# Two moves in a pipelined loop: one block transpose behind the last low part of h, and the fourth output scatter of each half step into that step

## The chip, the cores and the metric

The kernel runs on one core of a Trainium2 chip. The metric is device time in microseconds (us), from the start to the end of one launch. Before the change the median of three runs is 740.99 us (740.6 to 742.04). The engines are named as in the profile: PE (TensorE matmul), PEld (its weight loads), DVE (VectorE), ACT (ScalarE), POOL (GpSimd, which issues the DMAs that gather or scatter rows by an index list) and SP (which issues the plain DMAs).

## The reference

The reference has two parts. The first is an attention over columns; its result, read as 20,224 tokens of 256 features, goes into a routed two-layer network with 8 experts.

```python
def _attn_ref(q, k, v, tau):                      # q, k, v: 4 x 5056 x 256
    qn = q / (np.linalg.norm(q, axis=1, keepdims=True) + 1e-06)
    kn = k / (np.linalg.norm(k, axis=1, keepdims=True) + 1e-06)
    s = kn.transpose(0, 2, 1) @ qn / tau
    s = s - s.max(-1, keepdims=True)
    a = np.exp(s)
    a /= a.sum(-1, keepdims=True) + 1e-09
    return (v @ a).astype(np.float32)

def _moe_ref(x, w_skip, w_gate, w1, w2):          # x: 20224 x 256, F = 1024
    do_compute = x @ w_skip > 0
    out = x.copy()
    xc = x[do_compute]
    logits = xc @ w_gate
    e_idx = np.argmax(logits, axis=1)
    gate_w = ...                                  # softmax of logits at e_idx
    for e in range(8):
        mask = e_idx == e
        h = np.maximum(xc[mask] @ w1[e], 0.0)
        y[mask] = gate_w[mask, None] * (h @ w2[e])
    out[do_compute] = xc + y
    return out
```

The change concerns only the last part: for chunks of tokens of one expert, `h = relu(x w1)`, `y = h w2`, and `out = x + gate * y`, written back to the rows that the tokens came from.

## The kernel before

The attention, the routing and the first nine chunks of the network run ahead of the loop that the change touches. Their order is written by a planner (a table of costs and due times); the nine chunks run "ahead", between the products of the attention. Then comes `Large.loop()`, with five passes of two chunks each. A chunk is 512 tokens of one expert in four tiles (t = 0 to 3) of 128 tokens. A last loop for small remainders makes no pass here.

A chunk goes through these steps. `take` copies its index list, `gather` fetches its 512 rows into `xg` with four indirect DMAs from POOL (`gather_tile`, L235). `turned` makes two block transposes of `xg` into `xt` on DVE (L320), one for each half of the 256 features; SP writes them to a scratch in memory and reads them back as `xT` (`moved_out`, L323, and `moved_in`, L326), and `split_x` splits `xT` into a high and a low part, `xH` and `xL`. `first` computes `ph = x w1` for eight blocks f of 128 hidden features (three matmuls for each of two feature halves, L380 to L382). For each f ACT writes the high part `hH` (L385) and DVE the low part `hL` (L386). `second` computes for each tile t the product with `w2`: eight matmuls with `hH` (L406), then eight with `hL` (L408). DVE multiplies by the gate and adds `x` (L413, L414) into the buffer `xg[2]`, and `put(2, t)` scatters the 128 rows of the tile to `out` with one indirect DMA from POOL (L240). The index list that the puts read is a copy of its own, `lc[2]`, made by `take_out` on POOL (L426).

A pass has four stages. Stages 0 and 1 hold `first` of half 1 (all in `first(True, 1)`, in which the second weights are split as well) and `second(0, t)`; stages 2 and 3 hold `first(False, 0)` and `second(1, t)`. So the halves are offset: while one half is in `second`, the list and rows for another are already fetched. Before each `tc.stage_boundary()` every engine has a place in its program called `behind(...)`. An engine enters the next stage only when all five engines have come past their `behind` in the stage ahead of it. The program has a semaphore for each of the four boundaries. PE's first matmul of `second(1, 0)` waits for the semaphore `sem_stage_1`, to which POOL contributes behind `take_out(1)` in stage 2. Between stages an engine runs its own instructions in the order in which they are written; POOL is a single queue of takes, gathers, puts and weight gathers (`gather_w`, L247), each waiting for what it needs.

In the kernel before, three of the four puts of a half step stand in the stage in which the tile is computed, except in stage 1, which holds all four; the fourth put of `second(1, t)` is `put_last()`, and stands in stage 0 of the next pass, behind the four gathers. After the last pass one more `put_last()` stands behind the loop. The last of the nine chunks ahead has three puts in the planner's table, and its fourth is the `put_last()` of the first pass. In `first`, for h = 0, both block transposes (`turned`) stand between the matmuls of the last block, f = 7, and its `first_h`, so DVE runs them ahead of the last `hL`. For h = 1 they stand behind everything.

Of the kernel before, what the change touches and what calls it, by code (L numbers as in the profile page):

```python
# [29 lines left out]
NFB = F // P  # L30
# [9 lines left out]
K0 = 9  # L40
# [121 lines left out]
def attn_moe(ctx: ExitStack, tc: tile.TileContext, q, k, vt, tau, w_skip, w_gate, w1, w2, out):  # L162
# [95 lines left out]
    def behind(*engines):  # L258

        for e in engines:  # L260
            tc.previous_stage_wait(e.engine)
# [7 lines left out]
    class Large:  # L269
# [118 lines left out]
        def first(self, new, h):  # L388

            for f in range(NFB):  # L390
                ph = psum["h"].tile([P, 512], F32, name="ph")
                self.first_p(ph, f)
                if f == NFB - 1 and h == 0:
                    self.turned(h)
                self.first_h(ph, f)
                if new and f < 4:
                    self.split_w2(f)
                if f == 4:
                    behind(T, S, V)
            if h == 1:  # L400
                self.turned(h)
# [127 lines left out]
        def loop(self):  # L529
            with tc.For_i(0, self.n, 1, iteration_sync="staggered", hint_engines=(mybir.EngineType.PE,)) as i, tc.manual_schedule():  # L530
                V.tensor_copy(self.wc, self.wii[:, ds(i + 1, 1)])
                V.tensor_copy(self.wd, self.wii[:, ds(i + 1, 1)])
                self.take(1)
                behind(G, SP)
                self.gather(1)
                self.put_last()
                gather_w(w1, self.w1r, self.wc)
                self.take_out(0)
                self.first(True, 1)
                tc.stage_boundary()  # L540
                self.moved_out()
                load_list(self.adi, i + 1, self.lN[:, :8, :], 8)
                gather_w(w2, self.w2r, self.wd)
                self.moved_in()
                for t in range(4):
                    self.second(0, t)
                    if t == 1:
                        behind(T, S, V, G, SP)
                        self.split_x()
                tc.stage_boundary()  # L550
                self.take(0)
                self.gather(0)
                self.take_out(1)
                behind(G, SP)
                self.first(False, 0)
                tc.stage_boundary()
                self.moved_out()
                self.moved_in()
                for t in range(4):
                    if t < 2:  # L560
                        self.split_w1(2 * t)
                        self.split_w1(2 * t + 1)
                    self.second(1, t, t < 3)
                    if t == 1:
                        self.split_x()
                        behind(T, S, V, G, SP)
            self.put_last()

    class Small:

# [563 lines left out]
    for c in range(NC):  # L1134
        b, ch = divmod(c, NCH)
        ld, users = {}, ([], [])
        for h in range(2):
            for j0, j1 in [(0, 2), (2, JH)] if c == 0 and h == 0 else [(0, JH)]:
                t = then("qk", add("D", 0.76 * (j1 - j0), lambda c=c, h=h, j0=j0, j1=j1: load_qk(c, h, j0, j1), due=1e9 if c else -99, hold=("part", 99) if j0 else ("qk", NQ)))
# [26 lines left out]
        for j in range(J):  # L1166
# [3 lines left out]
            t = then("A", add("T", 0.73 if (c, j // JH) in SPLIT else 0.873, lambda g=g: next(g), deps, nominal["A", c, j]))  # L1170
# [34 lines left out]
    for d in range(NC):  # L1205
# [10 lines left out]
        for j in range(J // 2):  # L1216
            t = then("B", add("T", 1.49, None, [sv[j > 2][1], sv[j >= 2][1], ready_a[b]], nominal["B", d, j], hold=("px", 2, 1)))
# [92 lines left out]
    for x in range(K0):  # L1310
        for i in range(4):
            gt = then("gat", add("G", 1.31 if i else 1.9, lambda x=x, i=i: large.gather_ahead(x, i), [lstA if x < KA else lstB, puts.get(x - 3)]))
            gt.rush = 0.0 if x else RUSH
            gd = add("D", 0.36, None, [gt])
        gd.slack = SLACK if x else 0.0
        tr = moved_last = rows_ready(x, gd)
        if x:
            for t in tr:
                t.due = nominal["H", x - 1, 4]
        for i in range(4):  # L1320
            g = large.first_ahead(2 * i)
            t = then("H", add("T", 2.74, None, tr + w1s[1::2], nominal["H", x, i], hold=("px", 2, 1)))
            t.f = lambda g=g, t=t: product(g, t)
            t.users, a = [], None
            for n in range(2):
                a = add("S", 0.6, lambda g=g, n=n: g.send((n, 0)), [t, done.get(x - 1), a])
                t.users.append(add("V", 0.69, lambda g=g, n=n: g.send((n, 1)), [a]))
            in_order["hL", i] = t.users
        last_m1 = t
        vs2 = []  # L1330
        for i in range(2 if x < K0 - 1 else 1):
            g = large.second_ahead(x, 2 * i)
            t = then("H", add("T", 5.65, None, [v for n in range(4) for v in in_order["hL", n]] + w2s[1::2], nominal["H", x, 4 + i], hold=("px", 2, 1)))
            t.early = {id(v): 0.69 * n for n in range(4) for v in in_order["hL", n]}
            t.f = lambda g=g, t=t: product(g, t)
            t.users = chain(g, ("V", 1.92), deps=[t])
            vs2 += t.users * 2
        for i in (2, 3) if x == K0 - 1 else ():
            def alone(x=x, i=i):
                po = psum["x"].tile([P, 2, 512], F32, name="px")[:, 0, :] if i == 2 else psum["t"].tile([P, 512], F32, name="pt")  # L1340
                yield from large.second_alone(x, i, po)
            g = alone()
            t = then("H", add("T", 2.82, None, [], nominal["H", x, 5], hold=("px", 2, 1) if i == 2 else ("pt", 1)))
            t.f = (lambda g=g, t=t: product(g, t)) if i == 2 else lambda g=g: next(g)
            t.users = chain(g, ("V", 0.99), deps=[t])
            vs2 += t.users
        done[x] = t
        for i in range(4 if x < K0 - 1 else 3):
            pt = then("put", add("G", 1.31, lambda x=x, i=i: large.put_ahead(x, i), [vs2[i]], nominal["H", x, 5] + 39))
            puts[x] = add("D", 0.36, None, [pt], nominal["H", x, 5] + 41)  # L1350

# [7 lines left out]
    t = based[NC - 1]  # L1359
    for n, cost in enumerate((1.6, 1.4, 1.7, 0.77, 2.05, 0.82, 1.58, 2.81, 0.87)):  # L1360
        t = add("V", cost, table_part, [t])
# [33 lines left out]
    for at, p in enumerate(TAILS):  # L1395
# [20 lines left out]
        f = steps("tail_transposed")  # L1416
        t = add("T", 0.3, f, [tgd, wg1], nominal["T", p, 0] - 6, hold=("pt", 1))
        c = add("S", 0.4, f, [t, firsts.get(older)])
        t.users = [c]
        f = steps("tail_first")  # L1420
        t = firsts[p] = add("T", 3.5, None, [c, *tw[0]], nominal["T", p, 1], hold=("px", 2, 1))
# [4 lines left out]
        f = steps("tail_turned")  # L1426
        t = turned[p] = add("T", 0.9, None, [r1], nominal["T", p, 2], hold=("px", 2, 1))
# [4 lines left out]
        f = steps("tail_second")  # L1432
        t = tails[p] = add("T", 3.5, None, [c0, c1, *tw[1]], nominal["T", p, 3], hold=("px", 2, 1))
# [80 lines left out]
```

## Time and profile before

The profile is of one execution that took 743.1 us; its span, from the first instruction to the last, is 741.4 us.

| what | before |
|---|---|
| median of three runs | 740.99 us (740.6 to 742.04) |
| the profiled execution | 743.1 us |
| its span | 741.4 us |
| PE busy | 727.0 us, 98% of the span |
| PEld busy | 632.1 us, 85% |
| DVE busy | 516.5 us, 70% |
| POOL busy | 393.7 us, 53% |
| ACT busy | 340.1 us, 46% |
| scatters by L240 | 76 (36 of the chunks ahead, 40 of the loop) |

The busy shares are over the whole launch. The loop is its last third, from 510.5 to 734.8 us, and the shares are others there. PE's slices on the page show nine tenths or more in every slice but the first and the last, and the granted clock is at its full level throughout.

### The profile page before, as it was taken

How to read it: one execution, taken by the hardware profiler on the slowest of the kernel's cores; microseconds unless marked ns; L12 is line 12 of the kernel's file. 1: busy time of each engine (PE TensorE's matmuls, PEld its weight loads, DVE VectorE, ACT ScalarE, POOL GpSimd, SP SyncE). 2: the span in 40 equal slices, each digit the busy share in tenths (PEclk: the TensorE clock that was granted, in tenths of full speed). 3: DMA queues.
4: the chain of work that ended last, by engine and by line, in shares of the span. 5: the costliest groups of instructions: out<-in, count | busy, mean ns of one | idle time of the engine just before them, and what ended most of it. 6: DMA issues, size and time to landing. Idle time of an engine off the chain costs nothing. (4 is left out here: it accounts for less than half of the span.)

```text
span 741.4 us, 12542 instructions
## 1 busy us (share of the span) xinstructions
PE 727.0 (98%) x4234; PEld 632.1 (85%) x4234; DVE 516.5 (70%) x1022; ACT 340.1 (46%) x515; POOL 393.7 (53%) x412
## 2 busy tenths in 40 slices
PE   7999999999999999999999999999999999999996
PEld 6899999999999888988888886578888888888885
DVE  4859989988887885674746883146566675767755
ACT  5668778767847542442412222233233442334422
POOL 4000188888887777786676653324345354344542
PEclk9999999999999999999999999999999999999999
DMA  8989989899676446642525748941332223233122
GB/s 355 368 317 364 369 297 370 258 393 376 207 256 227 127 144 172 215 146 85 159 73 141 280 160 297 380 152 50 89 110 79 99 85 94 97 107 99 56 85 87
DMA packets 85188, 145.05 MB, mean 196 GB/s; under 512 B 20554, under 2 KB 60264, under 8 KB 82832
## 3 DMA queue, kind: packets, MB, share of 16 engines
q1 hardware_dynamic: 68960, 119.74, 46.4%
q0 software_dynamic: 15200, 24.00, 10.2%
q10 hardware_dynamic: 976, 0.67, 0.3%
q8 instruction: 27, 0.44, 0.2%
q14 instruction: 25, 0.20, 0.1%
HBM read 115.71 MB, written 42.70 MB: 214 GB/s over the span
## 5 line engine op out<-in xcount | busy, mean ns | idle before, releaser
L1015 POOL DMA_INDIRECT lst<-pay,r_posi x160 | 190.2, 1188 | 131.6 <-DVE r_posi L1012 79.7
L240 POOL DMA_INDIRECT out<-xg,lc x76 | 78.1, 1027 | 125.9 <-DVE xg L414 75.0
L861 PE MATMUL s<-qt,kt 128*128 128x256 f32 x580 | 136.9, 387 | 5.0 <-DMA kt<-in_k 5.0
L861 PEld LDWEIGHTS s<-qt,kt 128*128 128x128 f32 x580 | 108.9, 194 | 18.4 <-DMA kt<-in_k 5.0
L235 POOL DMA_INDIRECT xg<-out,lc x80 | 83.6, 1044 | 35.1 <-issue 28.9
L934 PE MATMUL px<-aH,vH 128*128 128x266 f32 x320 | 99.0, 309 | 0.0
L935 PE MATMUL px<-aL,vH 128*128 128x266 f32 x320 | 91.5, 286 | 0.0
L936 PE MATMUL px<-aH,vL 128*128 128x266 f32 x320 | 91.4, 286 | 0.0
L385 ACT ACTIVATE hH<-ph 128x512 fp32r<-128x512 f32 x80 | 47.8, 598 | 83.9 <-PE ph L382 83.9
L941 ACT COPY xo<-px 128x532 f32<-128x532 f32 x80 | 48.1, 602 | 70.4 <-PE px L936 69.6
L406 PE MATMUL po<-w2s,hH 128*128 128x512 f32 x320 | 79.9, 392 | 0.0
L386 DVE SCALAR_TENSOR_TENSOR hL<-ph,hH 128x512 fp32r<-128x512 f32 x80 | 55.1, 688 | 35.5 <-ACT hH L385 34.3
L489 ACT ACTIVATE hH<-px 128x512 fp32r<-128x512 f32 x72 | 39.5, 596 | 85.0 <-PE px L382 85.0
L406 PE MATMUL px<-w2s,hH 128*128 128x512 f32 x280 | 70.3, 393 | 0.0
L491 DVE SCALAR_TENSOR_TENSOR hL<-px,hH 128x512 fp32r<-128x512 f32 x72 | 46.3, 682 | 31.4 <-ACT hH L489 31.2
L406 PEld LDWEIGHTS po<-w2s,hH 128*128 128x128 f32 x320 | 58.2, 189 | 10.8
L380 PE MATMUL ph<-xH,w1H 128*128 128x512 f32 x160 | 62.5, 390 | 0.8 <-PE m L1453 0.8
L381 PE MATMUL ph<-xL,w1H 128*128 128x512 f32 x160 | 62.4, 390 | 0.0
L382 PE MATMUL ph<-xH,w1L 128*128 128x512 f32 x160 | 62.3, 389 | 0.0
L935 PEld LDWEIGHTS px<-aL,vH 128*128 128x128 f32 x320 | 60.7, 190 | 1.3
L934 PEld LDWEIGHTS px<-aH,vH 128*128 128x128 f32 x320 | 60.5, 189 | 1.2
L936 PEld LDWEIGHTS px<-aH,vL 128*128 128x128 f32 x320 | 60.3, 188 | 0.0
(252 smaller groups left out, 1397.4 us busy)
## 6 DMA issues: line engine op xcount, KB each, us to landing
vf<-in_vt SPq DMA_DIRECT2D x32, 640.0 KB, 6.1
qt<-in_q SPq DMA_DIRECT2D x31, 640.0 KB, 7.7
kt<-in_k SPq DMA_DIRECT2D x31, 640.0 KB, 7.9
out<-xo SPq DMA_DIRECT2D x12, 1280.0 KB, 6.8
turn<-xt SPq DMA_DIRECT2D x38, 256.0 KB, 2.0
xT<-turn SPq DMA_DIRECT2D x38, 256.0 KB, 3.7
v1r<-in_w SPq DMA_DIRECT2D x8, 1024.0 KB, 9.6
v2r<-in_w SPq DMA_DIRECT2D x8, 1024.0 KB, 7.3
```

What stands on the lines that cost most here:

```text
L235: apart(G.indirect_dma_start(out=to, out_offset=None, in_=out[0:n, :], in_offset=IndirectOffsetOnAxis(ap=ls[:, 0:1], axis=0), bounds_check ...
L240: i = (G.indirect_dma_start(out=out, out_offset=IndirectOffsetOnAxis(ap=ls[:, 0:1], axis=0), in_=src, in_offset=None, bounds_check=NTOK - ...
L380: T.matmul(ph, self.w1H[:, fs], self.xH[:, kb, :], start=(kb == 0), stop=False)
L381: T.matmul(ph, self.w1H[:, fs], self.xL[:, kb, :], start=False, stop=False)
L382: T.matmul(ph, self.w1L[:, fs], self.xH[:, kb, :], start=False, stop=(kb == 1))
L386: V.scalar_tensor_tensor(self.hL[:, f, :], ph, 0.0, self.hH[:, f, :], ALU.max, ALU.subtract)
L406: T.matmul(po, self.hH[:, f, ts], self.w2s[:, f, :, :], start=(f == 0), stop=False, skip_group_check=True)
L861: T.matmul(sums[b][:, cb, :], kt[:, j % JH, cb * P : (cb + 1) * P], qt[:, j % JH, :], start=(ch == 0 and j == 0 and cb == 0), stop=(ch == ...
L934: T.matmul(px[:, i, :NA], vH[:, kb, js], aH[:, kb, :], start=(kb == 0), stop=False)
L935: T.matmul(px[:, i, :NA], vH[:, kb, js], aL[:, kb, :], start=False, stop=False)
L936: T.matmul(px[:, i, :NA], vL[:, kb, js], aH[:, kb, :], start=False, stop=(kb == 1))
L1015: i = G.indirect_dma_start(out=lst, out_offset=IndirectOffsetOnAxis(ap=posi[:, t : t + 1], axis=0), in_=pay[:, d, 2 * t : 2 * t + W], in_o ...
```

## The change

Two things move, and no operation is added or taken away. The first is in `first`, for h = 0: of the two block transposes one stays ahead of the last `first_h`, and one now stands behind it. The second concerns the fourth puts. That of the first half's step, `second(0, 3)`, leaves stage 1 and stands in stage 2, behind the four gathers and ahead of `take_out(1)`. That of the second half's step, `second(1, 3)`, now stands in stage 3 with the other three, so the `put_last()` in stage 0 and the one behind the loop go. The last chunk ahead gets its fourth put in the planner's table, ahead of the loop.

```diff
--- before.py
+++ after.py
@@ -391,8 +391,10 @@
                 ph = psum["h"].tile([P, 512], F32, name="ph")
                 self.first_p(ph, f)
                 if f == NFB - 1 and h == 0:
-                    self.turned(h)
+                    self.turned_part(h, 0)
                 self.first_h(ph, f)
+                if f == NFB - 1 and h == 0:
+                    self.turned_part(h, 1)
                 if new and f < 4:
                     self.split_w2(f)
                 if f == 4:
@@ -533,7 +535,6 @@
                 self.take(1)
                 behind(G, SP)
                 self.gather(1)
-                self.put_last()
                 gather_w(w1, self.w1r, self.wc)
                 self.take_out(0)
                 self.first(True, 1)
@@ -543,13 +544,14 @@
                 gather_w(w2, self.w2r, self.wd)
                 self.moved_in()
                 for t in range(4):
-                    self.second(0, t)
+                    self.second(0, t, t < 3)
                     if t == 1:
                         behind(T, S, V, G, SP)
                         self.split_x()
                 tc.stage_boundary()
                 self.take(0)
                 self.gather(0)
+                self.put_last()
                 self.take_out(1)
                 behind(G, SP)
                 self.first(False, 0)
@@ -560,11 +562,10 @@
                     if t < 2:
                         self.split_w1(2 * t)
                         self.split_w1(2 * t + 1)
-                    self.second(1, t, t < 3)
+                    self.second(1, t)
                     if t == 1:
                         self.split_x()
                         behind(T, S, V, G, SP)
-            self.put_last()
 
     class Small:
 
@@ -1345,7 +1346,7 @@
             t.users = chain(g, ("V", 0.99), deps=[t])
             vs2 += t.users
         done[x] = t
-        for i in range(4 if x < K0 - 1 else 3):
+        for i in range(4):
             pt = then("put", add("G", 1.31, lambda x=x, i=i: large.put_ahead(x, i), [vs2[i]], nominal["H", x, 5] + 39))
             puts[x] = add("D", 0.36, None, [pt], nominal["H", x, 5] + 41)
 
```

The first place is POOL's queue at the turn from stage 1 to stage 2. `xg_152` is the buffer of results and `lc_162` the puts' index list; `xg_150` and `lc_160` are the rows and list being fetched. Names such as `DMASW4_..._stg1` are semaphores by which an earlier software DMA of that stage reports that it has landed, and `sem_stage_1` marks the boundary to stage 3. POOL before:

```order
L240 DMA out<-xg_152,lc_162 20224x256 [waits DVE_I-5912_stg1]
L530 ISA [waits sem_stage_0_7432]
L299 COPY lc_160<-lN 128x8 [waits DMAHW2_I-5912_stg1]
L235 DMA xg_150<-out,lc_160 128x256 [waits Pool_I-5912_stg2]
L235 DMA xg_150<-out,lc_160 128x256 x3
L426 COPY lc_162<-lc_161 128x8 [waits DMASW3_I-5912_stg1,DMASW4_I-5912_stg1,DMASW2_I-5912_stg1,DMASW1_I-5912_stg1]
L530 ISA [waits DMASW4_I-5912_stg1,DMASW0_I-5912_stg1,DMASW3_I-5912_stg1,DMASW1_I-5912_stg1,DMASW2_I-5912_stg1,sem_stage_1_7433]
```

POOL after, the same stretch:

```order
L240 DMA out<-xg_152,lc_162 20224x256 [waits DMASW4_I-5915_stg0,DMASW3_I-5915_stg0,Pool_I-5915_stg0,DMASW2_I-5915_stg0,DMASW0_I-5915_stg0,DMASW1_I-5915_stg0,DVE_I-5915_stg1]
L532 ISA [waits sem_stage_0_7432]
L299 COPY lc_160<-lN 128x8 [waits DMAHW2_I-5915_stg1]
L235 DMA xg_150<-out,lc_160 128x256 [waits Pool_I-5915_stg2]
L235 DMA xg_150<-out,lc_160 128x256 x2
L235 DMA xg_150<-out,lc_160 128x256 [waits DVE_I-5915_stg1]
L240 DMA out<-xg_152,lc_162 20224x256 [waits DVE_I-5915_stg1]
L428 COPY lc_162<-lc_161 128x8 [waits DMASW3_I-5915_stg1,DMASW4_I-5915_stg2,DMASW2_I-5915_stg1,DMASW1_I-5915_stg1]
L532 ISA [waits DMASW0_I-5915_stg1,DMASW3_I-5915_stg1,DMASW1_I-5915_stg1,DMASW2_I-5915_stg1,sem_stage_1_7433]
```

The fourth put has moved from ahead of the stage boundary to behind the gathers, the fourth gather has a wait for DVE that it did not have, and the copy L426 (now L428), `take_out(1)`, waits for the landing of a DMA of stage 2, the put just ahead of it, where it waited for one of stage 1.

The second place is POOL's queue at the entry of the loop. The `ISA` rows that follow the puts belong to the loop's entry, and the one with `barrier_...` is the wait for all engines. POOL before:

```order
L240 DMA out<-xg_152,lc_162 20224x256 [waits DMASW0_49,DVE_49]
L240 DMA out<-xg_152,lc_162 20224x256 [waits DMASW1_49,DVE_49]
L240 DMA out<-xg_152,lc_162 20224x256 [waits DMASW2_49,DVE_49]
L530 ISA x2
L530 ISA [waits barrier_Pool_Activation_PE_DVE_SP_gather,DMASW5_49,DMASW4_49,DMASW3_49]
```

POOL after:

```order
L240 DMA out<-xg_152,lc_162 20224x256 [waits DMASW0_49,DVE_49]
L240 DMA out<-xg_152,lc_162 20224x256 [waits DMASW1_49,DVE_49]
L240 DMA out<-xg_152,lc_162 20224x256 [waits DMASW2_49,DVE_49]
L240 DMA out<-xg_152,lc_162 20224x256 [waits DMASW3_49,DVE_49]
L532 ISA x2
L532 ISA [waits barrier_Pool_Activation_PE_DVE_SP_gather,DMASW6_49,DMASW7_49,DMASW5_49,DMASW4_49]
```

Four puts of the last chunk ahead stand there where three stood, and the entry follows behind the fourth.

The third place is DVE's queue in `first(False, 0)`, stage 2, from the first block f = 0 to the last; `xt_2575` and `xt_2576` are the two transposed halves. DVE before:

```order
L386 SCALAR_TENSOR_TENSOR hL<-ph,hH 128x512 [waits sem_stage_0_7432,Activation_I-5912_stg2]
L386 SCALAR_TENSOR_TENSOR hL<-ph,hH 128x512 [waits Activation_I-5912_stg2] x4
L386 SCALAR_TENSOR_TENSOR hL<-ph,hH 128x512 [waits DVE_I-5912_stg1,Activation_I-5912_stg2]
L386 SCALAR_TENSOR_TENSOR hL<-ph,hH 128x512 [waits Activation_I-5912_stg2]
L320 STREAM_TRANSPOSE xt_2575<-xg_150 128x4x4x32 [waits DMASW2_I-5912_stg2,DMASW1_I-5912_stg2,DMASW3_I-5912_stg2,DMASW0_I-5912_stg2,DMAHW0_I-5912_stg1]
L320 STREAM_TRANSPOSE xt_2576<-xg_150 128x4x4x32 [waits DMAHW1_I-5912_stg1]
L386 SCALAR_TENSOR_TENSOR hL<-ph,hH 128x512 [waits Activation_I-5912_stg2]
```

DVE after:

```order
L386 SCALAR_TENSOR_TENSOR hL<-ph,hH 128x512 [waits sem_stage_0_7432,Activation_I-5915_stg2]
L386 SCALAR_TENSOR_TENSOR hL<-ph,hH 128x512 [waits Activation_I-5915_stg2] x4
L386 SCALAR_TENSOR_TENSOR hL<-ph,hH 128x512 [waits DVE_I-5915_stg1,Activation_I-5915_stg2]
L386 SCALAR_TENSOR_TENSOR hL<-ph,hH 128x512 [waits Activation_I-5915_stg2]
L320 STREAM_TRANSPOSE xt_2575<-xg_150 128x4x4x32 [waits DMASW2_I-5915_stg2,DMASW1_I-5915_stg2,DMASW3_I-5915_stg2,DMASW0_I-5915_stg2,DMAHW0_I-5915_stg1]
L386 SCALAR_TENSOR_TENSOR hL<-ph,hH 128x512 [waits Activation_I-5915_stg2]
L320 STREAM_TRANSPOSE xt_2576<-xg_150 128x4x4x32 [waits DMAHW1_I-5915_stg1]
```

The last `hL` row stood behind both transposes and now stands between them.

## Rows read from the trace of the kernel before

**Rows 1.** Busy by stretch: sum, PE, PEld, DVE, ACT, POOL, clock, DMA, GB/s.

```profile
510.50:734.80 224.30, 222.18 (x1120) 188.76 (x1120) 149.06 (x248) 80.70 (x140) 97.05 (x110) 1.00 0.29 91
```

**Rows 2.** Waits of PEld in the loop: us, count, longest of one.

```profile
PEld po L408 <- DVE hL L386: 3.0, 5, 0.8
```

**Rows 3.** Timeline, PEld: start, busy, what, [idle before, releaser]; passes 4 and 5.

```profile
677.98 1.77 PEld L406 LDWEIGHTS po<-w2s,hH 128*128 128x128 f32 x8
...
681.55 0.19 PEld L408 LDWEIGHTS po<-w2s,hL 128*128 128x128 f32 x1 [0.74 <-DVE hL L386]
...
722.89 1.77 PEld L406 LDWEIGHTS po<-w2s,hH 128*128 128x128 f32 x8
```

**Rows 4.** Timeline, DVE, the end of first(False, 0) in pass 4.

```profile
678.80 2.12 DVE L320 STREAM_TRANSPOSE xt<-xg 128x512 f32<-128x512 f32 x2 [0.38 <-DMA xg<-out,lc]
680.82 0.67 DVE L386 SCALAR_TENSOR_TENSOR hL<-ph,hH 128x512 fp32r<-128x512 f32 x1
```

**Rows 5.** Timeline, POOL, stages 1 and 2 of pass 4, and put 2 of pass 5.

```profile
669.21 0.98 POOL L240 DMA_INDIRECT out<-xg,lc  x1 [4.96 <-DVE xg L414]
670.50 0.97 POOL L240 DMA_INDIRECT out<-xg,lc  x1 [0.30 <-issue]
...
671.95 1.07 POOL L235 DMA_INDIRECT xg<-out,lc  x1 [0.27 <-POOL lc L299]
...
675.95 0.99 POOL L235 DMA_INDIRECT xg<-out,lc  x1 [0.30 <-issue]
676.95 0.20 POOL L426 COPY lc<-lc 128x8 int32<-128x8 int32 x1
...
713.83 0.97 POOL L240 DMA_INDIRECT out<-xg,lc  x1 [4.65 <-DVE xg L414]
```

**Rows 6.** Timeline, POOL, put_last and take_out(0) in stage 0 of pass 4.

```profile
652.98 1.01 POOL L240 DMA_INDIRECT out<-xg,lc  x1 [0.30 <-issue]
...
655.58 0.19 POOL L426 COPY lc<-lc 128x8 int32<-128x8 int32 x1 [0.25 <-DMA out<-xg,lc]
```

**Rows 7.** Timeline, POOL, DVE and PE at the turn from pass 3 to 4.

```profile
643.92 0.97 POOL L240 DMA_INDIRECT out<-xg,lc  x1 [1.61 <-DVE xg L414]
...
647.68 1.06 POOL L235 DMA_INDIRECT xg<-out,lc  x1 [2.59 <-issue]
...
645.96 0.48 DVE L414 SCALAR_TENSOR_TENSOR xg<-po,lc,xg 128x256 f32<-128x256 f32 x1
...
657.64 1.10 DVE L320 STREAM_TRANSPOSE xt<-xg 128x512 f32<-128x512 f32 x1
...
667.33 0.69 DVE L350 TENSOR_TENSOR xL<-xT,xH 128x512 fp32r<-128x512 f32 x1 [0.69 <-ACT xH L348]
...
668.22 0.39 PE L381 MATMUL ph<-xL,w1H 128*128 128x512 f32 x1
```

**Rows 8.** Timeline and one line's events (ns min/median/max, first, last) at loop entry.

```profile
507.20 0.97 POOL L240 DMA_INDIRECT out<-xg,lc  x1 [0.35 <-DVE xg L414]
...
L530 POOLq INC_SWDGE_SEM  x2: 535/562/588, 507.1 to 507.7; - x2
L530 POOLq EVENT_SEMAPHORE  x1: 17/17/17, 509.4 to 509.4; - x1
...
506.44 0.48 DVE L414 SCALAR_TENSOR_TENSOR xg<-px,lc,xg 128x256 f32<-128x256 f32 x1
...
509.07 0.48 DVE L414 SCALAR_TENSOR_TENSOR xg<-pt,lc,xg 128x256 f32<-128x256 f32 x1
...
510.54 0.47 PE L380 MATMUL ph<-xH,w1H 128*128 128x512 f32 x1 [0.76 <-PE m L1453]
```

**Rows 9.** Timeline and PE's sequencer at the end of the program.

```profile
735.30 0.48 DVE L414 SCALAR_TENSOR_TENSOR xg<-po,lc,xg 128x256 f32<-128x256 f32 x1
...
736.75 0.97 POOL L240 DMA_INDIRECT out<-xg,lc  x1 [2.50 <-POOLq L1468]
...
L1468 PEldq COMPARE_BRANCH  x1: 3535/3535/3535, 736.0 to 736.0; - x1
```

## The prediction

> **What bounds the kernel now.** I read the table of the page first, then busy time by stretch, then the waits of PEld inside the loop, then the timelines of POOL, DVE and PE around each moved instruction. In the loop PE is busy 222.18 of 224.30 us [rows 1], so in the loop each end is set by PE, and what is to be gained is 2.1 us plus whatever PE's own work could save, which the change does not touch. The view of waits says where these 2 us lie: PEld's load of a slice of `hL` (L408) waits for DVE's L386 3.0 us in all, once in each of the five passes, about 0.6 us each [rows 2]. (The weight loads run ahead of the matmuls, so PE itself shows a little less.) The reader should see in the timeline that it is the eighth L408 load of `second(1, 0)`: it sits 0.74 us for the last `hL` [rows 3], which DVE wrote behind both transposes [rows 4]. Everything else is off PE's path at present, POOL above all: before put 2 of stage 1 it stands idle 4.96 and 4.65 us [rows 5]. But POOL stands in the path indirectly, by the stage boundaries, and that is where the second half of the change acts.
>
> **The transpose behind the last low part.** Before, the two transposes run 678.80 to 680.92, with 0.38 us of DMA wait ahead of them, and the last L386 begins at 680.82 [rows 4]. After, only one transpose of some 1.06 us stands ahead of it, and the fourth gather comes 1.28 us earlier (below), so the DMA wait goes too. `hL` is then ready at about 678.42 + 1.06 + 0.67 - 0.10 (the overlap that the rows show) = 680.05, where PEld first wanted it at 681.55 - 0.74 = 680.81 [rows 3]. The wait goes: 3.0 us over five passes, and nothing is late behind it, since that load is then followed by loads that need no later data. I take -3.0, with -2.4 as the near end (PE does not show the whole of PEld's wait; PE's idle time in the loop is 224.30 - 222.18 = 2.1, of which 0.8 is at the entry [rows 1, 8], but a matmul that overlaps its neighbour counts twice in the busy sum, so that bound is loose) and -3.7 as the far one (five times the 0.74). The second transpose, 0.7 us later than now at most, feeds `split_x` in stage 3, whose result is wanted behind all four tiles of `second`; in the last pass these take from 722.89 to the loop's end at 734.8 [rows 1, 3], 11.9 us. Cost 0.
>
> **The first half's fourth put in stage 2.** This is the term that decides. PE's first matmul of `second(1, 0)` waits for `sem_stage_1`, that is until POOL is past its place behind `take_out(1)`. Before, POOL reached that copy, L426, at 676.95, right behind the last gather's issue and without a wait, 1.03 us ahead of PE's load at 677.98 [rows 3, 5]. After, the same copy stands behind a put, and has to wait until that put has read its index list and landed. What that takes the trace shows elsewhere: in stage 0 a put starts at 652.98, and the copy L426 that waits for it runs at 655.58, 2.60 us after the put's start and after an idle of 0.25 us that the landing of that put ended [rows 6]. Now the start of the put. Without the fourth put in stage 1, the `take` and the gathers follow put 2 directly: put 2 at 669.21, fourth put 670.50, first gather 671.95, fourth gather 675.95, copy 676.95 [rows 5]. One put less is 1.29 us, so the fourth gather goes to about 674.67 and the fourth put, one step of 1.3 us further, to 675.97, which is 6.76 us behind put 2; copy at 678.57, 9.36 behind put 2. Its own run and the signal to PE's queue I take as 0.27 us, between 0.13 and 0.4 (the copy lasts 0.20 [rows 6]): PE is let in 9.63 us behind put 2. It wants in at 677.98, which is 8.77 behind in pass 4, and at 722.89, 9.06 behind put 2 at 713.83, in pass 5 [rows 3, 5]. Over the five passes the distance is 8.77 to 9.06; I take 8.9. So PE comes 0.73 us late at each pass, 5 x 0.73 = **+3.7 us**. Bounds: 0.46 (9.52 - 9.06) gives 2.3, and 1.0 (9.77 - 8.77) gives 5.0. If the put released its list at issue instead of at landing it would be nothing; the copy's release in the row is a DMA, so I don't take that. In the same stage the late start also moves the eighth L408 load back by about what it used to wait: the old wait of 0.6 to 0.74 and the new one are of one size, in the same stage.
>
> The Trainium skill, page "DMA: Bandwidth & Descriptors", section "Anatomy of one DMA — SWDGE (gpsimd) path", gives such a transfer about 2.0 us plus its bytes at 436 GB/s. For a put of 131 KB that is an estimate of 2.3 us where the row says 2.60 to the waiting copy; by the page the wait would be 0.3 shorter each time, this term 2.2 and the total 742.0 us. The row is of this kernel and includes what the copy waits for, so the row stands.
>
> The fourth gather's new wait (for DVE's reading of the tile that it overwrites) costs nothing: the old put 3, which needs that tile finished as well, ran 1.29 us behind put 2, and the fourth gather stands 5.46 us behind it (674.67 - 669.21) [rows 5].
>
> **The second half's fourth put in stage 3.** `put_last` leaves stage 0, where it stood between the gathers and `w1r` without holding anyone. Now the first gather of the next pass is behind it: it has to see that put landed. The put follows DVE's L414 of tile 3, which ends at 645.96 + 0.48 = 646.44, by 0.28 (as 507.20 follows 506.44 + 0.48 [rows 8]), so at 646.72. Between the last put that it waits for and the first gather there are now 647.68 - 643.92 = 3.76 us, with an idle of 2.59 in them [rows 7]; that makes 650.48 for the gather. From the first gather to the fourth are 4.00 us (671.95 to 675.95 [rows 5]), and a fourth gather at 675.95 let the transposes begin at 678.80, 2.85 later [rows 4, 5]. So the rows are there at 657.33, and DVE's transpose starts at 657.64 [rows 7]. The cover is 0.3 us, thin. Behind it is another: `xL` ends 667.33 + 0.69 = 668.02 and PE uses it at 668.22 [rows 7], a further 0.2. So cost 0, upper end +1 in all.
>
> **The loop's entry.** The fourth put of the last chunk ahead now stands before the barrier of all engines that opens the loop. Before, POOL is early: put at 507.20 and the two `INC_SWDGE_SEM` of 0.59 and 0.54 us by 508.2, then it waits for DVE's arrival until 509.4 [rows 8]. After, the put waits for L414, 509.07 + 0.48 = 509.55, and the same chain follows. Between the end of its L414 (506.92) and its own at 508.24 it took 1.32, so POOL arrives at 510.87, 1.5 us later than the barrier opened before. PE started its first L380 at 510.54, after an idle 0.76 [rows 8]; that idle becomes 2.26. I take **+1.5** (1.3 to 1.7; 0 if the put's instructions were not ahead of the arrival, but the order shows them there).
>
> **The end.** The last put stood behind the exit barrier: 736.75, after an idle 2.50 released by the branch [rows 9]. After, it comes at 735.30 + 0.48 + 0.28 = 736.06, 0.7 earlier, but POOL, and with it the barrier, comes up to that put's 0.97 us later, and PE's closing branch of 3.535 us, begun at 736.0 [rows 9], starts later. I take +0.3 (between -0.7 and +0.3).
>
> **Sum.** +1.5 + 3.7 - 3.0 + 0 + 0.3 = +2.5 us on the profiled execution of 743.1 us, thus 745.6. The median of the runs, 740.99, lies 2.1 below that execution; by the same difference I predict **743.5 us**.
>
> **Rivals.**
> 1. Faster, the other side: PE never meets the boundary. Its place is the same turn from stage 2 to 3, and it decides if the copy comes within 2.1 us of the put's start instead of 2.6 (8.90 - 6.76 = 2.14). Then -3.0 + 1.5 + 0.2 = -1.3, 739.7 us; without the entry's term as well, 738.2. For it: the put would meet less traffic there than in stage 0, where the weight gathers go. Against: the release is by landing, and no put to copy distance in the rows is near 2.1. Chance 0.16, of which a little more than half falls under 739.5.
> 2. Cancelled: the stage wait is at its lower end (2.3 us), or half of the entry's delay is made good. Then +2.3 + 0.8 - 3.0 + 0.2 = +0.3, 741.3 us. For it: the two waits are of one size and in one stage. Against: the distances 8.77 to 9.06 are steady. Chance 0.17.
> 3. The gathers of stage 0 come late: the cover of 0.3 us at the transposes is gone, PE waits for `xL` at each of five turns. With 0.4 each it is 2 us more, 745.5 us. For it: the thin slack. Against: two covers in a row. Chance 0.08.
>
> The forecast has the remaining 0.59.
>
> **How the numbers follow.** A difference of 0.2%, 1.5 us, is about the least that a measurement of this kernel tells from none: faster is under 739.5, slower above 742.5. Faster has 0.09 of rival 1. Same has the other 0.07, 0.15 of rival 2 and 0.06 of the forecast (its terms at their low ends together, 2.3 + 1.3 - 3.7 - 0.7, come to -0.8), 0.28. Slower has the remainder, 0.63. The range goes from 739.6, where the first rival with its entry term lies, to 745.6, the third rival; the forecast's own goes from 742.1 to 744.8 (the sum with 2.3 or 5.0 for its largest term).
>
> **What would show it.** In the trace after: L408 no longer waits for L386 at the end of stage 2 (first term). PEld's first L406 of each `second(1, 0)` shows an idle of 0.5 to 1.0 us, put down to POOL or to the boundary, with the copy L428 2.6 us behind the put (second term). POOL's copy with an idle ahead of it by a DMA. PE's first matmul of the loop with 2.2 us idle (entry). DVE's transposes in stage 0 no later than now against PE (third rival wrong). If that L406 has no idle time the forecast is wrong, and the kernel is faster.

## The result: 0.5% slower, and the profile after

The changed kernel takes 745.66 us (median of five runs, 744.2 to 747.21); the kernel before took 741.37 us beside it (740.6 to 742.05). The ratio is 1.0053, with a 95% interval from 1.0043 to 1.0064, which is +3.9 us (3.2 to 4.7) on 741.37. In a second comparison it was 745.59 against 741.58, ratio 1.0058 (1.0045 to 1.0072). The forecast was slower by 2.5 us, at 743.5, with a range up to 745.6, which is +4.6 on the 740.99 that it went out from. The sign and the mechanisms are as forecast. The amount, +4.3 and +4.0 as differences of the medians, lies at the far end of the range, and past what the forecast's own terms reach (744.8, or +3.8). In the first four runs of the next section (the split alone for the first time, without the first half's move, a list of its own for the first time, without the split) the work ahead of the loop took some 64 to 77 us longer, in the kernel before too (806.8 us), so that their ratios (0.9975, 0.9992, 1.0038 and 1.0055, each within 0.5 to 0.7% either way) say nothing of a few us and only their loops are read.

The profiled execution took 745.66 us, with a span of 744.0 us against 741.4 before. All rows of this section are of the changed kernel, whose line numbers are two higher from `second_p` on (L406 is now L408, L408 is L410, L413 and L414 are L415 and L416, L426 is L428). The waits of PEld and of PE from the loop's entry to its end (us in all, times, the longest; PEld's own at the entry is left out):

```profile
PEld po L408 <- issue: 3.7, 5, 0.9
```

```profile
PE ph L380 <- PEq L532: 2.3, 1, 2.3
PE po L408 <- issue: 1.7, 4, 0.5
```

The reader should see what has gone and what has come. The load of `hL` (L410 now) no longer waits for L386 [rows 2]. In its place the first load of `second(1, 0)` waits in each of the five passes, 3.7 us in all, and "issue" means that the profile names no instruction as releaser: it is the stage boundary. PE, which runs behind its loads, shows 1.7 of it in four rows; the lengths of its stages, in the next section, make it 2.9 over all five. And the first matmul of the loop waits 2.3 us instead of 0.76 [rows 8].

The timeline of POOL and of PEld in stage 2 of pass 4 shows why (start, busy, what, and the idle time before it with its releaser):

```profile
676.75 0.99 POOL L235 DMA_INDIRECT xg<-out,lc  x1 [0.30 <-issue]
678.05 1.02 POOL L240 DMA_INDIRECT out<-xg,lc  x1 [0.30 <-issue]
680.66 0.18 POOL L428 COPY lc<-lc 128x8 int32<-128x8 int32 x1 [1.59 <-DMA out<-xg,lc]
...
681.06 1.67 PEld L408 LDWEIGHTS po<-w2s,hH 128*128 128x128 f32 x8 [0.88 <-issue]
```

The put starts 1.30 us behind the fourth gather; the copy of `take_out(1)` waits for it to land and runs 2.61 us behind the put's start; PE's load comes 0.40 us behind the copy. Before, the copy stood right behind the fourth gather and PE came 1.03 us after it without a wait [rows 3, 5].

The turn to the next pass. POOL's last put of pass 3, its first and fourth gathers, and DVE's transposes:

```profile
649.03 0.97 POOL L240 DMA_INDIRECT out<-xg,lc  x1 [1.88 <-DVE xg L416]
...
652.81 1.06 POOL L235 DMA_INDIRECT xg<-out,lc  x1 [2.60 <-issue]
...
656.80 0.99 POOL L235 DMA_INDIRECT xg<-out,lc  x1 [0.30 <-issue]
```

```profile
659.27 0.69 DVE L386 SCALAR_TENSOR_TENSOR hL<-ph,hH 128x512 fp32r<-128x512 f32 x1 [0.67 <-ACT hH L385]
659.88 2.09 DVE L320 STREAM_TRANSPOSE xt<-xg 128x512 f32<-128x512 f32 x2
```

The gather comes 3.78 us behind the put, as between the same two instructions before (3.76) [rows 7]. The transposes start 3.08 us behind the fourth gather with no idle time ahead of them, straight behind the last `hL`: the rows were there (the gather landed about 2.7 us behind its start), with little to spare.

The loop's entry, first DVE's last add ahead of it and the put that waits for it, then PE, and then each stretch (length, PE, PEld, DVE, ACT and POOL busy, the granted clock, the DMA share and GB/s):

```profile
508.52 0.48 DVE L416 SCALAR_TENSOR_TENSOR xg<-pt,lc,xg 128x256 f32<-128x256 f32 x1
...
509.28 0.97 POOL L240 DMA_INDIRECT out<-xg,lc  x1 [1.66 <-DVE xg L416]
...
511.51 0.65 PE L380 MATMUL ph<-xH,w1H 128*128 128x512 f32 x1 [2.29 <-PEq L532]
...
513.24 0.63 PE L381 MATMUL ph<-xL,w1H 128*128 128x512 f32 x1
...
515.23 0.39 PE L380 MATMUL ph<-xH,w1H 128*128 128x512 f32 x1
```

```profile
505.00:509.00 4.00, 4.00 (x29) 3.67 (x28) 2.31 (x5) 0.00 (x0) 2.27 (x2) 1.00 0.27 98
509.00:511.50 2.50, 0.23 (x3) 0.05 (x2) 0.29 (x2) 0.00 (x0) 0.97 (x1) 1.00 0.15 52
...
511.65:515.06 3.41, 3.41 (x9) 2.67 (x10) 0.02 (x1) 0.65 (x2) 1.25 (x2) 0.50 0.03 7
...
516.00:518.00 2.00, 2.00 (x11) 1.63 (x10) 1.57 (x3) 1.59 (x3) 1.39 (x3) 1.00 0.27 84
```

Two things are to be seen. DVE's last L416 ended at 508.52 + 0.48 = 509.00 here, so PE's first matmul comes 2.51 us behind it, where it came 0.99 behind it before (510.54 - 509.55) [rows 8]: the entry is 1.52 us longer. And behind that idle time TensorE's granted clock is 0.50, the lower of its two levels, from 511.65 to 515.06. The matmuls last 0.63 instead of 0.39 us there, and `first` of the first pass takes 12.60 us from its start to that of the next stage, against 11.00 before. That 1.6 us was in no term of the forecast.

The end of the program, DVE's last add, POOL's last put and PE's closing branch:

```profile
737.50 0.48 DVE L416 SCALAR_TENSOR_TENSOR xg<-po,lc,xg 128x256 f32<-128x256 f32 x1
...
738.26 0.98 POOL L240 DMA_INDIRECT out<-xg,lc  x1 [1.89 <-DVE xg L416]
...
L1469 PEldq COMPARE_BRANCH  x1: 3675/3675/3675, 739.3 to 739.3; - x1
```

The put comes 0.28 us behind L416 as forecast. The branch starts 1.3 us behind the end of L416 where it started 0.2 behind it before [rows 9], but the last put, which came only behind the exit barrier before, is done earlier, and at the end of the span 0.5 us are left of the 1.1 (it ends 7.17 us behind PE's last matmul, against 6.67).

### The profile page after: what moved, and what is told of

It reads as the page before. It is cut to its first block, busy times and chain, and to the rows that moved or that the text cites. A ratio compares the mean times of both kernels' runs of the same rounds, so it can differ in the third digit from the quotient of the medians.

```text
span 744.0 us, 12548 instructions
## 1 busy us (share of the span) xinstructions
PE 727.8 (98%) x4234; PEld 632.1 (85%) x4234; DVE 516.3 (69%) x1022; ACT 340.1 (46%) x515; POOL 393.7 (53%) x412
## 5 line engine op out<-in xcount | busy, mean ns | idle before, releaser
L408 PE MATMUL po<-w2s,hH 128*128 128x512 f32 x320 | 80.3, 393 | 1.7 <-issue 1.7
L386 DVE SCALAR_TENSOR_TENSOR hL<-ph,hH 128x512 fp32r<-128x512 f32 x80 | 55.1, 689 | 37.6 <-ACT hH L385 36.4
L408 PE MATMUL px<-w2s,hH 128*128 128x512 f32 x280 | 70.3, 393 | 0.0
L408 PEld LDWEIGHTS po<-w2s,hH 128*128 128x128 f32 x320 | 57.8, 189 | 14.2 <-issue 3.7
L380 PE MATMUL ph<-xH,w1H 128*128 128x512 f32 x160 | 63.1, 394 | 2.3 <-PEq L532 2.3
```

The costliest lines, as they stand in the source:

```text
L380: T.matmul(ph, self.w1H[:, fs], self.xH[:, kb, :], start=(kb == 0), stop=False)
L386: V.scalar_tensor_tensor(self.hL[:, f, :], ph, 0.0, self.hH[:, f, :], ALU.max, ALU.subtract)
L408: T.matmul(po, self.hH[:, f, ts], self.w2s[:, f, :, :], start=(f == 0), stop=False, skip_group_check=True)
```

## The experiments

To set the runs side by side, three lengths are read from PE's timeline in each trace: the idle time ahead of the loop's first L380; the length of the loop, from that start to the end of the last matmul of `second(1, 3)`; and the lengths of the stages, from the first matmul of one to that of the next. An undisturbed `first` takes 10.91 us, an undisturbed `second` 11.15 (11.30 for the last one, up to the end of its last matmul). All lengths are in us.

| kernel | idle at the entry | loop | its first `first` | `first(False, 0)`, over 10.91, five passes | `second(1, ...)`, over 11.15 (last 11.30), five passes |
|---|---|---|---|---|---|
| before, the profiled execution | 0.76 | 224.21 | 11.00 | 0.0 | 3.4 |
| before, three more | 0.76 to 0.79 | 223.39, 223.05, 222.96 | 11.0 | 0.0 | 2.6, 2.3, 2.2 |
| the whole change, twice | 2.29, 2.31 | 225.36, 225.38 | 12.60, 12.51 | 2.5 | 0.4, 0.5 |
| the split of the transposes alone, twice | 0.76, 0.76 | 220.90, 220.93 | 11.0 | 0.0 | 0.1, 0.2 |
| without the first half's move | 2.28 | 220.78 | 11.00 | 0.0 | 0.0 |
| a list of its own, twice | 2.31, 2.32 | 222.47, 220.83 | 12.60, 10.98 | 0.1 | 0.0 |
| without the split | 2.28 | 224.47 | 10.96 | 3.2 | 0.5 |
| without the last put ahead | 0.79 | 223.94 | 10.99 | 2.6 | 0.5 |

**The split of the transposes alone.**

```diff
--- before
+++ the split alone
                 if f == NFB - 1 and h == 0:
-                    self.turned(h)
+                    self.turned_part(h, 0)
                 self.first_h(ph, f)
+                if f == NFB - 1 and h == 0:
+                    self.turned_part(h, 1)
```

Expected the first time: 

> The kernel before with one part of the change alone: one block transpose behind the last low part of h; all puts stand where they stood. Theory (the parts add up as the traces show): second(1, ...) of a pass lasted 11.99, 11.98, 11.72, 11.95 and 11.62 us on PE before and 11.15 is what second(0, ...) lasts, so the late low part costs PE 3.5 us, a little more than the 3.0 of PEld's wait. They go, nothing else comes: 741.4 - 3.5 = 737.9 us, ratio 0.995; entry idle 0.8 us at the full clock, no wait of the first L406 of second(1, 0). Rival (the transpose is needed where it stood, or the gain was already paid by something else): the wait turns up elsewhere, 740.5 to 741.5 us.

Expected the second time: 

> The kernel before with the split of the transposes alone, timed once more, since in the first timing the part ahead of the loop varied by 25 us in every kernel. Theory (the five waits for the last low part go and nothing replaces them; the first trace shows all five second(1, ...) at 11.15 us): 3.5 us less than before, ratio 0.995, clear of 1. Rival (the loop's gain is given back ahead of or behind the loop): ratio 0.998 to 1.002.

Measured: 739.44 us against 741.58, ratio 0.9972 (0.9962 to 0.9983), 2.1 us faster (1.3 to 2.8). It has the lowest median of the kernels here. In the loop neither PE nor PEld has a wait that the views list. The timeline of DVE and PEld in pass 4 of the second run:

```profile
675.76 1.08 DVE L320 STREAM_TRANSPOSE xt<-xg 128x512 f32<-128x512 f32 x1
676.77 0.65 DVE L386 SCALAR_TENSOR_TENSOR hL<-ph,hH 128x512 fp32r<-128x512 f32 x1
677.34 1.13 DVE L320 STREAM_TRANSPOSE xt<-xg 128x512 f32<-128x512 f32 x1
```

```profile
677.22 1.13 PEld L410 LDWEIGHTS po<-w2s,hL 128*128 128x128 f32 x8
```

The last `hL` ends at 677.42, and the eight loads that read `hL` run in one piece; the last of them, the only one that needs the last `hL`, starts some 0.19 us ahead of their end at 678.35, well behind 677.42. So this part does what it was forecast to do. But the median moved by 2.1 us and not by the 3.5 expected from the traces, and the upper end of the interval, 0.9983, just reaches into the rival's band. No loss is seen where the rival puts it, though: the program ends 6.63 us behind PE's last matmul, as before (6.67), and the loop starts at 510.10, within the 508.8 to 510.5 of the four traces of before. Three more executions of before, below, say more on the size.

**The first half's put back in stage 1.**

```diff
--- the changed kernel
+++ without the first half's move
-                    self.second(0, t, t < 3)
+                    self.second(0, t)
...
                 self.gather(0)
-                self.put_last()
                 self.take_out(1)
```

Expected: 

> The changed kernel with the first half's fourth put back in stage 1 (transpose split, second half's put in stage 3 and the fourth put ahead of the loop stay). Theory: the boundary wait goes (2.5 us between the stages and 0.4 in them, 2.9 in all), the entry stays with its 2.3 us of idle time and the low clock behind it: 745.5 - 2.9 = 742.6 us, and no idle time ahead of PE's first matmul of second(1, 0). Rival (the boundary wait takes the place of something else and hides it): 745 us, with a new wait in second(1, ...).

Measured in its trace: the loop takes 220.78 us, the shortest of all, and no `first(False, 0)` is longer than 10.91. PE's only wait there is the entry's (the view of waits, from shortly ahead of the loop):

```profile
PE ph L380 <- PEq L532: 2.3, 1, 2.3
```

So the wait at the boundary comes from this move alone, and the rival, a new wait in `second(1, ...)`, does not appear. The low clock did not follow the idle time here, though that was as long as in the changed kernel.

**A list of its own for the second half's puts.** The put stays behind the fourth gather; `take_out(1)` writes a fourth list, `lc[3]`, which no put in flight reads.

```diff
--- the changed kernel
+++ a list of its own
-            self.lc = [rows([P, 4, 2], I32, name=f"lc{h}") for h in range(3)]
+            self.lc = [rows([P, 4, 2], I32, name=f"lc{h}") for h in range(4)]
...
-            self.second_x(po, h, t, 2)
+            self.second_x(po, h, t, 2, 2 + h)
             if out:
-                self.put(2, t)
+                scatter_x(self.lc[2 + h][:, t, :], self.xg[2][:, t, :])
...
-            G.tensor_copy(self.lc[2], self.lc[h])
+            G.tensor_copy(self.lc[2 + h], self.lc[h])
```

Expected the first time: 

> The changed kernel, but the second half has an index list of its own for its puts, so that take_out(1) writes another buffer than the one that the put ahead of it reads; the put stays where the change has it, behind the fourth gather. Theory (it is the wait for that put's landing, not its place or its traffic): the copy follows the put at once, about 1.3 us behind it and not 2.6, POOL is past its place about as early as before, the boundary wait goes: 742.6 us, like the run with that put back in stage 1. Rival (the place or the traffic of the put costs the time): 745 to 745.5 us, idle time of 0.5 us ahead of second(1, 0) as in the changed kernel.

Expected the second time: 

> The changed kernel with an index list of its own for the second half's puts, timed once more. Theory (the first trace shows no boundary wait and all second(1, ...) at 11.15 us or less): 2.9 us less than the whole change, 0 to 1.5 us slower than before by the entry's idle time and clock, ratio 1.000 to 1.0015. Rival (the copy's wait was only moved to another place): ratio 1.003 to 1.005.

Measured: 742.61 us against 741.58, ratio 1.0012 (1.0002 to 1.0022), 3.0 us less than the whole change beside it. POOL in pass 4 of the second run, and PEld:

```profile
673.06 0.99 POOL L235 DMA_INDIRECT xg<-out,lc  x1 [0.30 <-issue]
674.36 1.02 POOL L240 DMA_INDIRECT out<-xg,lc  x1 [0.30 <-issue]
675.38 0.20 POOL L428 COPY lc<-lc 128x8 int32<-128x8 int32 x1
```

```profile
676.50 1.77 PEld L408 LDWEIGHTS po<-w2s,hH 128*128 128x128 f32 x8
```

The put stands where the change has it, 1.30 us behind the gather, and goes out to the same rows. But the copy follows at 1.02 us without an idle, and PEld enters `second(1, 0)` without a wait. So neither the place nor the traffic of the put costs the 3 us: it is the wait for its landing, forced by the one shared list.

**The moves of the puts without the split.**

```diff
--- the changed kernel
+++ without the split
-                    self.turned_part(h, 0)
+                    self.turned(h)
                 self.first_h(ph, f)
-                if f == NFB - 1 and h == 0:
-                    self.turned_part(h, 1)
```

Expected: 

> The changed kernel with both transposes ahead of the last low part again; the moves of the puts stay. Theory (the boundary wait and the wait for the low part overlap): PE enters second(1, 0) some 0.55 us late, and wants the last low part that much later; the gathers come 1.28 us earlier, so the low part comes 0.4 us earlier too, so it is no longer waited for, or by 0.1 us at most. The split is worth 0 to 0.5 us here: 745.5 to 746 us. Rival (the two waits add up): 745.5 + 3.5 = 749 us, with both an idle 0.5 ahead of second(1, 0) and one of 0.6 in it.

Measured in its trace (PEld's waits inside the loop):

```profile
PEld po L406 <- issue: 4.0, 5, 1.0
PEld ph L381 <- DVE xL L350: 0.5, 1, 0.5
```

There is no wait for `hL`, as the theory had it. The loop takes 224.47 us at the full clock, while the changed kernel's takes 225.36 with 1.6 us of low clock in it, 223.8 without: 0.7 us more, not 3.5. But some 0.5 us of that is no matter of the last `hL`: in pass 2 `first(False, 0)` is 1.15 us too long, of which the boundary makes 0.63, and the rest goes with the load that waits 0.5 us for `xL`. That is the wait of the prediction's third rival, once. It leaves about 0.2 us for the split, less than one execution differs from another, and there is one trace of this kernel. So with the put in stage 2 the boundary lets PE in so late that the last `hL` is finished in any case. The two waits overlap; each is worth its full price only without the other.

**Without the last put ahead of the loop.** This run doesn't write the 128 rows of that put; else it is the changed kernel.

```diff
--- the changed kernel
+++ without the last put ahead
-        for i in range(4):
+        for i in range(4 if x < K0 - 1 else 3):
```

Expected: 

> The changed kernel without the fourth put of the last chunk ahead of the loop: 128 rows of the output are not written. Theory (that put holds the barrier at the loop's entry): PE idles 0.8 us at the entry as before, its first eight blocks run at the full clock, POOL's part of the entry is over by the time DVE arrives; 1.5 us less than the whole change, and 1.6 more where that falls to the low clock: 0 to 1 us slower than before, ratio 1.000 to 1.0015. Rival (the entry waits for something else that the change moved): idle 2.3 us stays, ratio 1.003 to 1.005.

Measured: 742.97 us against 741.58, ratio 1.0019 (1.0009 to 1.0028), 2.6 us less than the whole change beside it. PE at the entry:

```profile
508.79 0.28 PE L1454 MATMUL m<-ones 128*128 128x128 f32 x1
509.86 0.47 PE L380 MATMUL ph<-xH,w1H 128*128 128x512 f32 x1 [0.79 <-PE m L1454]
```

The idle time is 0.79 us again, as before the change, and the next matmuls run at the full clock. So this one put makes the entry longer: 1.5 us of idle time, and the rest of the 2.6 through the clock. The ratio is a little above the 1.0015 that was expected at most, though its interval holds that; before's loop is usually some 1.1 us shorter than the profiled one, as the last runs of this section show, and that would make the difference.

**The whole change once more.** Expected: 

> The changed kernel once more, beside its parts. Theory: 3 to 4 us slower than before (0.6 less in the loop, 1.5 of idle time at the entry, 1.6 of low clock behind it in some executions, 0.4 at the end): ratio 1.003 to 1.0055. Rival (the clock at the entry was a single event, and the 4 us of the first timing lie ahead of the loop): ratio 1.001 to 1.002.

Measured: 745.59 us, ratio 1.0058 (1.0045 to 1.0072), just above the expected 1.0055 and clear of the rival's 1.002. The entry's stretches in its trace and, for comparison, in that of the kernel with a list of its own (second run), which idles as long:

```profile
508.50:511.30 2.80, 0.49 (x5) 0.33 (x3) 0.44 (x3) 0.00 (x0) 0.97 (x1) 0.94 0.13 47
511.30:513.30 2.00, 2.00 (x5) 1.63 (x6) 0.00 (x0) 0.00 (x0) 0.19 (x1) 0.50 0.04 12
```

```profile
508.50:511.30 2.80, 0.49 (x5) 0.32 (x4) 0.55 (x3) 0.00 (x0) 0.97 (x1) 1.00 0.13 47
511.30:513.30 2.00, 2.00 (x9) 1.66 (x10) 0.00 (x0) 0.25 (x1) 0.19 (x1) 1.00 0.04 12
```

With the same PE work ahead and the same 2.8 us stretch, the clock is 0.50 behind the one and 1.00 behind the other: 5 matmuls against 9 in 2 us. The mean granted clock of each timed execution says how often that is. With the list of its own it is 0.995 in eight of twelve executions (742.26 to 743.60 us) and 0.997 or 0.998 in the other four (740.35 to 740.90 us); with the whole change it is 0.995 or 0.996 in eight of eleven. None of the 26 executions of before in the same comparison, and none of the twelve without the last put ahead, is under 0.997. So one and the same kernel, with the same idle time, runs with the low clock and without it: the code does not decide it. The two groups of the list of its own lie 2.3 us apart, more than the 1.6 that the traces show at the entry; the rest of that is not explained.

**Three more executions of the kernel before.** Expected: 

> The kernel before, one more execution with its trace. Open: the split alone took 3.3 us from the loop by the traces, but 2.1 us by the medians; the traced execution of before (743.1 us) lies above nearly all its timed ones. Theory (the wait for the last low part hangs on when the gathered rows land and differs between executions; it was large in the traced one): the five second(1, ...) lose less against 11.15 than the 3.5 us seen, 1.5 to 2.5 us in all, and the loop takes 222.3 to 223.3 us instead of 224.2. Rival (it is the part ahead of the loop that differs): the loop takes 224.0 to 224.4 us again.

Expected of the second and the third: 

> The same as the look before it: theory, a loop of 222.3 to 223.3 us; rival, 224.0 to 224.4 us.

 

> The same as the two looks before it: theory, a loop of 222.3 to 223.3 us; rival, 224.0 to 224.4 us.

Measured: 740.41, 740.49 and 740.60 us, with loops of 223.39, 223.05 and 222.96 us. The waits of PEld in the loop, one row from each of the three:

```profile
PEld po L408 <- DVE hL L386: 2.3, 5, 0.8
```

```profile
PEld po L408 <- DVE hL L386: 2.0, 5, 0.8
```

```profile
PEld po L408 <- DVE hL L386: 1.9, 5, 0.7
```

And DVE's wait ahead of the transposes for the gathered rows, first in the profiled execution of before, then in the three:

```profile
DVE xt L320 <- DMA xg<-out,lc: 1.4, 4, 0.4
```

```profile
DVE xt L320 <- DMA xg<-out,lc: 0.7, 2, 0.5
```

```profile
DVE xt L320 <- DMA xg<-out,lc: 0.4, 1, 0.4
```

```profile
DVE xt L320 <- DMA xg<-out,lc: 0.3, 1, 0.3
```

In all four executions PEld's wait [rows 2] is DVE's plus 1.6 us: 3.0 and 1.4, 2.3 and 0.7, 2.0 and 0.4, 1.9 and 0.3. So what differs is how late the gathered rows land, and 1.6 us is what the two transposes ahead of the last `hL` cost by themselves. The mean of the three loops is 223.1, against 220.9 with the split: 2.2 us, close to the 2.1 of the medians. One loop, 223.39, lies 0.1 us above what the theory allowed, but far from the rival's 224.0 to 224.4. The rival has a share all the same: these three loops start at 508.77 to 509.40, up to 1.8 us ahead of the profiled one's 510.54, so the part ahead of the loop differs between executions of one kernel by as much as the loop does, and the three lie some 1.1 us under before's median. The agreement of 2.2 with 2.1 is no closer than that.

## Why the prediction was right, and where its sizes were off

1. **The wait for the last low part goes: right, but worth 2.2 us and not 3.0.** The mechanism is shown by the split alone. The term took its size from one execution, in which the gathered rows came late in four of five passes; in the three others the wait is about 2 us.
2. **The boundary between stages 2 and 3: right, and 2.9 us on PE instead of 3.7.** The place, the landing (2.61 us from the put to the copy, 2.60 forecast) and PEld's 3.7 us in five waits are as worked out; the load comes 0.40 us behind the copy where 0.27 was taken. (The lower bound has a slip: 9.36 and 0.13 make 9.49, so 2.2 us and not 2.3; nothing hangs on it.) But the sum charged PE with the whole of PEld's wait, and PE lost 2.5 us between the stages and 0.4 in them. That fits loads that run ahead of their matmuls and have some slack before PE feels a delay; no run takes it apart. The list of its own shows that it is the landing. The estimate of 2.3 us from the Trainium skill (page "DMA: Bandwidth & Descriptors", section "Anatomy of one DMA — SWDGE (gpsimd) path") falls short: in the changed kernel's trace the put lands about 2.5 us behind its start, and the copy runs 2.61 behind it.
3. **The loop's entry: right in its idle time, 1.53 us for the forecast 1.5, and short of a term.** The step that failed is the sentence that the idle time becomes 2.26 us and costs 1.5: it priced the idle time alone. In both traces of the whole change the clock was at its lower level behind it, which cost another 1.5 to 1.6 us; the sum had nothing for that. The run without that put has neither. In the three of eleven executions of the whole change whose mean clock is 0.997 or 0.998, the time is 743.5, 744.2 and 745.0 us, on the average 2.7 above before's 741.58: close to the forecast's +2.5.
4. **The turn to the next pass: right, cost 0.** In both traces of the whole change nothing waits for the transposes, though they come behind a gather that is 3 us later.
5. **The end: +0.5 and +0.3 us in the two traces, for +0.3.** No run takes this term apart.

Put together with the measured sizes: -2.2 + 2.9 + 1.5 + 1.55 + 0.4 = +4.2 us, where the medians say +4.3 and +4.0. The forecast's +2.5 is short by the clock's 1.55 and by the 0.8 of the first term, and long by the 0.8 of the second. Rival 1, that PE never meets the boundary, is refuted by five waits in five passes; its price is what the list of its own shows: a loop of 220.8 us and 3.0 us less in all. Rival 2 named the right kinship of the two waits, but they nearly cancel in the loop alone (223.8 without the low clock against 223.1), and the entry came on top. Rival 3 did not occur in either trace of the whole change; its wait for `xL` shows once without the split (0.5 us) and once in the first trace of the list of its own (0.2 us), so the cover is as thin as the prediction said. The range reaches the measured amount only because rival 3's price set its upper end: that the number falls there is luck, for the amount came from the clock.

Open is what decides whether the clock falls behind the same 2.3 us of idle time: it did in three of six traces with that idle time (the whole change twice, the list of its own once), and in none of the seven with less than 0.8. In the three it fell between 0.2 us ahead of the loop's first matmul and 0.8 us behind its start.

## What to carry to other kernels

An instruction that only copies a small table can become the gate of a pipeline: before a DMA is moved ahead of it, look whether the copy overwrites what that DMA reads, and give each half a buffer of its own if it does. Two waits in one place need not add up, as here, so price a part both with and without the other. And take the size of a wait that ends on a DMA from several executions, not from the one that happens to be profiled.

## What the runs showed of the hardware

An idle time of 2.3 us on PE, with matmuls back to back behind it, was followed in three of six traces by 3.4 us at the lower level of the granted clock (0.50), in which a 128x512 matmul took 0.63 us instead of 0.39. `first` became 1.5 to 1.6 us longer by it, as much again as the added idle time itself cost.

A scatter of 128 rows from POOL landed about 2.5 us behind its start, and a copy that overwrites its index list ran 2.61 us behind that start; with a list of its own it ran at 1.02.
